# An adaLN decode block on one core: a quarter of w2's last row loaded apart, and all of w2 in calls of 128 columns

## The chip, the core and the metric

The kernel runs on one core of one Trainium2 chip. The metric is the device time of one execution in microseconds (us), the median of the runs shown. The kernel before took 235.53 us (three runs, 235.41 to 235.98). The profile is of one execution; its times count from its first instruction.

The engines are named as in the profile: PE (matrix multiply) with PEld (its loading of weights), DVE, ACT, POOL, and SP, which here only issues transfers. A "call" below is one matmul of the program. In float32 the chip runs each call as two passes, so the profile counts two matmuls for a call.

## The reference

One decode step for two rows: an attention branch over a window of 4096 cached positions, and a feed-forward branch, both modulated by a condition `c`. Cut to what matters:

```python
mod = (silu(c) @ w_mod).reshape(2, 6, 1, 512)
sa, ca, ga, sb, cb, gb = (mod[:, i] for i in range(6))
h = layernorm(x) * (1 + ca) + sa
x = x + ga * attention(h, k_cache, v_cache, wq, wo)   # 32 query heads, 8 KV heads of 128,
                                                      # the last 4096 of 32768 positions
h = layernorm(x) * (1 + cb) + sb
x = x + gb * (silu(h @ w1) @ w2)                      # w1: 512 x 1792, w2: 1792 x 512
```

`x` is 2 x 1 x 512. All arrays are float32.

## The kernel before

Everything is streamed once from HBM through `slots`, a ring of eight buffers of 128 partitions x 4096 numbers (`stream`, line 70). SP issues the loads in program order: w_mod, x, wq, then for eight steps the K and V rows of a pair of heads (`load_pair`, two buffers, 4 MB each), then wo in two loads, w1 in two, and w2 in four (`load_runs`). A load is issued when its buffer is free, so SP mostly waits, for the last reader of the buffer. `fetch(s)` asks for K of step s and V of step s - 1.

A step s: `keys` turns K on DVE, `scores` multiplies on PE, `maxima` and `exponentials` make the softmax, `turn` turns the weights, `weighted` multiplies V, `collect` adds the heads into `o_all`. `tc.keep_in_program_order` (`inorder`) fixes the order of the instructions it wraps; the rest is placed by a scheduler. `qbd[0]` and `qbd[1]` hold the queries, spread out over 128 x 1024 numbers; `qbd[0]` serves the heads of steps 0 to 3 alone.

The sums over heads are divided by the softmax's denominator (`rx`, `lp`, `rl`, `on`, lines 516 to 538), turned (`oTn`), and multiplied by wo. `busy(n)` puts n matmuls whose result nobody reads on PE.

The feed-forward branch at the end is what the change touches:

- The hidden vector has 1792 numbers, on 128 partitions x 14 (`T2`). `uT` holds it after SiLU, ready as weights: slice tt is `uT[:, tt, :]`, 32 columns of which two (columns 0 and 16) carry the two rows of the batch.
- Partition p of w2's buffers holds rows 14 p to 14 p + 13 of w2, so slice tt of w2 is one row of 512 on each partition. "The last row" is slice 13. The four loads bring slices 0 to 7, 8 to 10, 11 to 12, and 13.
- Slices 0 to 7 (`WIDE`) run as calls of 512 columns (line 663), four column groups of PE side by side: slice tt goes to partitions 32 g to 32 g + 31 of the bank `yw`, g = tt % 4. Each group then holds the sum of two slices over all 512 columns.
- Slices 8 to 10 run as four calls of 128 columns each (line 673): the g-th quarter of the columns goes to partitions 32 g and up of the bank `y`. This is the layout that the rest of the kernel has: batch row b's g-th quarter stands on partition 32 g + 16 b.
- `gather(y, yw, ...)` (lines 548 to 560, called in line 680) brings the wide sums into that layout: ACT and DVE copy one half of `yw` each to SBUF, and four calls with `id4` (which adds the four groups) put the quarters into `y`.
- Slices 11 to 13 run as calls of 64 columns into two banks `yl[0]`, `yl[1]` (line 688).
- DVE then multiplies `y` by `gb` and adds x1 (`yp`, lines 696 and 697), multiplies the two `yl` by `gb` (line 701), adds both (line 704), and SP stores `yo` (line 706).

PSUM banks are named by a tag; tag D has two buffers, used in turn.

Of the kernel before, what the change touches and what calls it, by code (L numbers as in the profile page):

```python
# [19 lines left out]
RING = 8  # L20


@with_exitstack
def adaln_block(
# [82 lines left out]
    for b in range(B):  # L107
# [55 lines left out]
        odd, ident.rearrange("p (a r) -> p r a", r=2), axis=AX.X, op=ALU.add  # L163
    )
# [434 lines left out]
    T2, WIDE = F // P, 8  # L599
# [60 lines left out]
    yw = bank("D", "acc_yw")  # L660
    for tt in range(WIDE):
        g = tt % 4
        inorder(nc.tensor.matmul(  # L663
            yw[32 * g : 32 * g + 32, :],
            uT[:, tt, :],
            w2t[tt],
            start=(tt < 4),
            stop=(tt >= WIDE - 4),
        ))
    y = bank("D", "acc_y")[:, :P]  # L670
    for tt in range(WIDE, 11):
        for g in range(4):
            inorder(nc.tensor.matmul(  # L673
                y[32 * g : 32 * g + 32, :],
                uT[:, tt, :],
                w2t[tt][:, g * P : (g + 1) * P],
                start=(tt == WIDE),
                stop=False,
            ))
    gather(y, yw, "acc_y_sb", False, True)  # L680
# [3 lines left out]
    for tt in range(11, T2):  # L684
        for h in range(2):
            for g in range(4):
                lo = g * P + h * H
                inorder(nc.tensor.matmul(
                    yl[h][32 * g : 32 * g + 32, :],
                    uT[:, tt, :],  # L690
                    w2t[tt][:, lo : lo + H],
                    start=(tt == 11),
                    stop=(tt == T2 - 1),
                ))
# [39 lines left out]
```

## Time and profile before

| | |
|---|---|
| median of three runs | 235.53 us |
| span of the profiled execution (first to last instruction) | 233.7 us |
| mean TensorE clock granted | 0.934 of full |
| read from HBM | 97.53 MB, 417 GB/s over the span |
| busy share: PE, PEld, DVE, ACT, POOL | 69%, 18%, 49%, 12%, 5% |
| last instruction of DVE ends, output's store is issued | 231.1 us |

The page gives no total time for the profiled execution; the median of the runs lies 1.8 us above its span, which is what lies around it. In the page's slices each digit is a tenth. A row of the chain of waits gives its start, its length and what ran or was waited for. A row of the timeline merges neighbouring instructions of one line: start, length from the first start to the last end, engine, line, operation, output <- inputs, shape, count, and in brackets the idle time before it with what ended it. "SPq" is the time at which SP issues a transfer. w1 and w2 both read as "in_B_w" there.

The chain of waits of the whole execution, by engine (share of the span):

```profile
DMA 60%; issue 17%; DVE 14%; PE 6%; POOL 1%; POOLq 0%; SPq 0%; ACT 0%; DVEq 0%
```

Waiting for transfers makes up most of it.

### The profile page before, as it was taken

Reading aid. Unit: us, or ns where it says so; the run is one execution under the profiler, and the core shown is the slowest. Engines: PE = TensorE matmul, PEld = TensorE weight load, DVE = VectorE, ACT = ScalarE, POOL = GpSimd, SP = SyncE. Lnnn points to the kernel's source line nnn. Section 1 sums busy time; section 2 is a strip of 40 time slices with the busy share of each in tenths; the row PEclk is TensorE's granted clock in tenths of the full one; section 3 lists DMA queues with packets and bytes.
Section 4 is the critical chain, followed back from the end, with each engine's and each line's share of the span. In section 5 each row is a group of like instructions: output and inputs, shape, how many; then the busy total and the mean of one; then the engine's idle time right before and its main releaser. Section 6 shows DMA issues by size and latency. Waiting matters only on the chain.

```text
span 233.7 us, 2571 instructions
## 1 busy us (share of the span) xinstructions
PE 160.2 (69%) x1070; PEld 43.1 (18%) x1070; DVE 115.6 (49%) x179; ACT 28.5 (12%) x64; POOL 10.6 (5%) x35
## 2 busy tenths in 40 slices
PE   0005916959577839787689759758769777869784
PEld 0001401211111111221111202201112122314223
DVE  3004140178795758696197189249559540101232
ACT  1100210000311120120210201111030031002020
POOL 8600010000000000000000000000000000000000
PEclk9999975879979997999979988999997999999999
DMA  7998998999999999999999999999999999989991
GB/s 269 446 520 381 426 471 359 440 443 428 415 421 449 440 443 421 421 423 449 443 437 426 415 429 449 437 437 429 404 444 443 437 423 471 446 362 427 423 412 57
DMA packets 3795, 97.68 MB, mean 418 GB/s; under 512 B 433, under 2 KB 457, under 8 KB 969
## 3 DMA queue, kind: packets, MB, share of 16 engines
q1 hardware_dynamic: 3768, 97.53, 97.2%
q8 instruction: 8, 0.13, 0.2%
q14 instruction: 3, 0.02, 0.0%
q10 hardware_dynamic: 16, 0.00, 0.0%
HBM read 97.53 MB, written 0.00 MB: 417 GB/s over the span
## 4 chain that ended last, share of the span: by engine, by line
DMA 60%; issue 17%; DVE 14%; PE 6%; POOL 1%; POOLq 0%; SPq 0%; ACT 0%; DVEq 0%
DMA slots<-in_A_k_cache_dram 22%; DMA slots<-in_A_wq_dram 14%; DMA slots<-in_B_w_dram 12%; DMA slots<-in_A_v_cache_dram 12%; DVE kT L363 11%; PE q L304 3%; PE o L450 2%; DVE zp L422 1%; PE acc_yw L663 1%; DVE xp L420 1%; PE acc_y L673 0%; DVE xc L102 0%; POOL qg L321 0%; DVE qT L317 0%; PE acc_y L554 0%
## 5 line engine op out<-in xcount | busy, mean ns | idle before, releaser
L363 DVE STREAM_TRANSPOSE kT<-slots 128x1024 f32<-128x1024 f32 x64 | 73.7, 1210 | 22.9 <-DMA slots<-in_A_k_cache_dram 22.8
L376 PE MATMUL s<-kT,qbd 128*32 128x512 f32 x256 | 68.5, 703 | 17.9 <-DVE kT L363 17.0
L450 PE MATMUL o<-slots,ptb 128*32 128x512 f32 x256 | 29.1, 595 | 2.2 <-DMA slots<-in_A_v_cache_dram 2.2
L376 PEld LDWEIGHTS s<-kT,qbd 128*32 128x32 f32 x256 | 9.8, 113 | 66.9 <-DVE kT L363 62.9
L271 PE MATMUL m_a<-slots,scT 128*32 128x256 f32 x32 | 4.4, 507 | 20.4 <-DVE scT L263 20.4
L304 PE MATMUL q<-slots,hq_T 128*32 128x512 f32 x64 | 9.7, 773 | 7.4 <-DMA slots<-in_A_wq_dram 7.4
L450 PEld LDWEIGHTS o<-slots,ptb 128*32 128x32 f32 x256 | 7.7, 109 | 16.7 <-issue 16.6
L406 ACT COPY bias<-bp 128x1 f32<-128x1 f32 x8 | 1.3, 159 | 75.8 <-PE bp L404 75.8
L386 DVE TENSOR_REDUCE mx<-s 128x1 f32<-128x512 f32 x8 | 5.5, 691 | 9.6 <-PE s L376 9.6
L567 PE MATMUL junk<-quad,id 128*32 128x512 f32 x22 | 10.2, 596 | 0.0
L437 ACT ACTIVATE ptb<-pT,odd 128x256 f32<-128x256 f32 x16 | 6.7, 472 | 26.0 <-PE pT L429 26.0
L422 DVE TENSOR_TENSOR zp<-xp,quarter 128x1024 f32<-128x1024 f32 x8 | 9.8, 1225 | 0.2
L429 PE MATMUL pT<-zp,mix 128*32 128x256 f32 x64 | 5.8, 438 | 4.0 <-DVE zp L422 4.0
L317 DVE STREAM_TRANSPOSE qT<-q 128x512 f32<-128x512 f32 x2 | 1.4, 717 | 13.5 <-PE q L304 12.0
L581 PE MATMUL acc_o<-slots,oTn 128*32 128x512 f32 x56 | 6.2, 593 | 2.3 <-DMA slots<-in_A_wo_dram 2.3
L460 ACT COPY ob<-o 128x512 f32<-128x512 f32 x8 | 4.7, 586 | 24.4 <-PE o L450 24.4
L552 DVE COPY acc_o_sb<-acc_o 128x256 f32<-128x256 f32 x1 | 0.4, 425 | 14.1 <-ACT acc_o_sb L551 14.1
L388 PE MATMUL mT<-ident,mx 128*1 128x128 f32 x16 | 3.0, 270 | 6.3 <-DVE mx L386 6.3
L420 DVE STREAM_TRANSPOSE xp<-pr 128x512 f32<-128x512 f32 x8 | 5.5, 685 | 3.4 <-ACT pr L408 3.4
L257 DVE STREAM_TRANSPOSE cT<-xc 128x128 f32<-128x128 f32 x1 | 0.4, 401 | 13.7 <-DMA xc<-in_c_dram 13.7
L274 PE MATMUL m_sp<-slots,scT 128*32 128x512 f32 x32 | 7.2, 730 | 0.0
L468 PE MATMUL o_all<-ob,selh 128*64 128x128 f32 x64 | 5.9, 313 | 0.8 <-ACT ob L460 0.8
(140 smaller groups left out, 93.7 us busy)
## 6 DMA issues: line engine op xcount, KB each, us to landing
slots<-in_A_k_cache_dram SPq DMA_DIRECT2D x8, 4096.0 KB, 27.6
slots<-in_A_v_cache_dram SPq DMA_DIRECT2D x8, 4096.0 KB, 27.7
slots<-in_w_mod_dram SPq DMA_DIRECT2D x1, 6144.0 KB, 17.2
slots<-in_A_wo_dram SPq DMA_DIRECT2D x1, 6144.0 KB
slots<-in_B_w_dram SPq DMA_DIRECT2D x1, 2688.0 KB
slots<-in_A_wo_dram SPq DMA_DIRECT2D x1, 2048.0 KB, 29.5
slots<-in_B_w_dram SPq DMA_DIRECT2D x1, 2048.0 KB
slots<-in_B_w_dram SPq DMA_DIRECT2D x1, 896.0 KB
```

Of the source, the lines that this page charges most:

```text
L274: nc.tensor.matmul(m_sp[r, :], scT[:, k, :], cd[:, g], start=(k == 0), stop=(k == 3))
L304: nc.tensor.matmul(q_ps[n][32 * g : 32 * g + 32, :], hq_T[:, k, :], wv[:, n, g], start=(k == 0), stop=(k == 3),)
L363: inorder(nc.vector.transpose(kT[s, j][:, 32 * c : 32 * c + 32, :], kt[s].rearrange("p (n j r) -> p j n r", j=4, r=32)[:, j, 32 * c : 32 * ...
L376: inorder(nc.tensor.matmul(s_ps[s][r : r + 32, :], qbd[h // 4][:, h % 4, b, j, :], kT[s, j][:, 32 * c : 32 * c + 32, e:32:2], start=(j == ...
L420: inorder(nc.vector.transpose(xp, pr[s]))
L422: inorder(nc.vector.tensor_mul(zp, xp[:, None, :, 0:16].to_broadcast([P, 4, 16, 16]), quarter[:, :, None, None].to_broadcast([P, 4, 16, 16 ...
L429: inorder(nc.tensor.matmul(tp[32 * i : 32 * i + 32, :], mix.rearrange("p v e -> p (v e)"), zp.rearrange("p y t x -> p (y t) x")[:, :, 4 * ...
L437: inorder(nc.scalar.activation(ptb[s % 2][:, :, e, :], tp.rearrange("p (w z) -> p w z", z=16), AF.Copy, scale=odd[:, e : e + 1],))
L450: inorder(nc.tensor.matmul(o_ps[s][r : r + 32, :], ptb[s % 2][:, w].rearrange("p e z -> p (e z)"), vt[s].rearrange("p (c w m f d) -> p c f ...
L468: inorder(nc.tensor.matmul(o_all[r : r + 64, :], selh[:, m, lo : lo + 2 * HQ], o_sb[s][:, m * DH : (m + 1) * DH], start=(s == 0 and m < 2) ...
L567: inorder(nc.tensor.matmul(junk[0:32, :], id4, quad.rearrange("p m y -> p (m y)"), start=True, stop=True,))
L581: inorder(nc.tensor.matmul(acc[32 * g : 32 * g + 32, :], oTn[:, q, :], wot[q], start=(q < 4), stop=(q >= 24),))
```

## The change

Three things, all in the feed-forward branch and its loads.

**A quarter of the last row is loaded apart.** Columns 384 to 511 of slice 13 (128 numbers on each of 128 partitions, 64 KB) no longer come with the last load, which becomes 128 x 384. They go to a tile `far` in the memory of `qbd[0]`, which is free after step 3, and which POOL clears first. Rows of partitions 8 to 127 go there in eight loads of 15 rows (`move`), to three partitions of `far` each with five rows one behind the other (`far[:, j]`, j = 0 to 4): 24 partitions, 0 to 11 and 32 to 43. The rows of partitions 0 to 7 (`own`) go to `far[:8, 5]`. The moves are issued between the K and V loads of the last steps and the loads of wo; the row of `own` after them.

**Their products have a bank of their own.** The rows no longer stand on the partitions of their hidden numbers, so these are moved too: DVE writes slice 13 of `uT` into six pairs of columns, each masked to the partitions that `far[:, j]` took (`uj`, with the mask `slot`), one call with the 0/1 matrix `away` carries them to the 24 and 8 partitions (`up`), DVE copies that into `uF`, and six calls multiply `uF[:, j]` by `far[:, j]` into the bank `yf`, in four column groups. ACT copies `yf` to SBUF, and one call with `id4` adds the four groups into the last quarter of `y`. `away` and `slot` are made at the start by POOL and DVE.

**All slices from 0 to 10 run in calls of 128 columns** (`narrow`) into `y`; `yw` and its `gather` are gone. The load of slices 0 to 7 is split in two of four slices. The calls of `up`, `yf` and `id4` stand between the narrow ones.

```diff
+NE, NR, NJ = 3, 4, 5
...
+    own = P - 2 * NR * NJ * NE
+    away, slot = const([P, 48], "away"), const([P, NJ + 1], "slot")
+    nc.gpsimd.memset(away, 0.0)
+    for h in range(2):
+        nc.vector.tensor_reduce(
+            away[:, 32 * h : 32 * h + NE * NR].rearrange("p (e r) -> p e r", e=NE),
+            ident[:, own + 60 * h : own + 60 * h + 60].rearrange(
+                "p (r j e) -> p e r j", r=NR, j=NJ
+            ),
+            axis=AX.X,
+            op=ALU.add,
+        )
+    nc.vector.tensor_add(away[:, :own], away[:, :own], ident[:, :own])
...
+    T2, WIDE = F // P, 8
+    w2p = w2.rearrange("(p t) e -> p t e", t=T2)
+    spare = qbd[0].rearrange("p s b j c -> p (s b j c)")
+    NS = NJ + 1
+    far = spare[:, : NS * P].rearrange("p (j m) -> p j m", j=NS)
+    uF = spare[:, NS * P : NS * (P + 32)].rearrange("p (j n) -> p j n", j=NS)
+    uj = spare[:, NS * (P + 32) : NS * (P + 32 + B)].rearrange("p (j b) -> p j b", j=NS)
+    moves = [(h, r) for h in range(2) for r in range(NR)]
+
+    def move():
+
+        if len(moves) == 2 * NR:
+            nc.gpsimd.memset(spare, 0.0)
+        h, r = moves.pop(0)
+        lo = own + 60 * h + NJ * NE * r
+        nc.sync.dma_start(
+            far[32 * h : 32 * h + NE * NR, :NJ].rearrange("(e r) j m -> e r j m", r=NR)[:, r],
+            w2p[lo : lo + NJ * NE, T2 - 1, D - P :].rearrange("(j e) m -> e j m", e=NE),
+        )
...
             kt[s] = load_pair(k_cache, s)
+            if s > STEPS // 2 + 1:
+                move()
         if s > 0:
             vt[s - 1] = load_pair(v_cache, s - 1)
+            if s > STEPS // 2:
+                move()
...
         wt = load_runs(wo, 32, lo, hi)
+        move()
         wot.extend(wt[:, q, :] for q in range(hi - lo))
+    nc.sync.dma_start(far[:own, NJ], w2p[:own, T2 - 1, D - P :])
...
-    for lo, hi in ((0, WIDE), (WIDE, 11), (11, 13), (13, T2)):
+    wide = stream(1).rearrange("p (q e) -> p q e", e=D)
+    for lo in (0, WIDE // 2):
+        nc.sync.dma_start(wide[:, lo : lo + WIDE // 2, :], w2p[:, lo : lo + WIDE // 2, :])
...
+    w2l = stream(1)[:, :D]
+    nc.sync.dma_start(w2l[:, : D - P], w2p[:, T2 - 1, : D - P])
...
-    yw = bank("D", "acc_yw")
-    for tt in range(WIDE):
...
-    gather(y, yw, "acc_y_sb", False, True)
+    nc.vector.tensor_mul(
+        uj,
+        uT[:, T2 - 1, 0:32:16][:, None, :].to_broadcast([P, NS, B]),
+        slot[:, :, None].to_broadcast([P, NS, B]),
+    )
...
+    narrow(0)
+    up = bank("C", "up")[:48, : NS * B]
+    inorder(nc.tensor.matmul(up, away, uj.rearrange("p j b -> p (j b)"), start=True, stop=True))
+    inorder(nc.vector.tensor_copy(
+        uF[:48, :, 0:32:16], up.rearrange("p (j b) -> p j b", b=B)
+    ))
+    for tt in range(1, 4):
+        narrow(tt)
+    yf = bank("D", "acc_yf")[:, :P]
+    for j in (4, 5, 0, 1, 2, 3):
+        g = j % 4
+        inorder(nc.tensor.matmul(
+            yf[32 * g : 32 * g + 32, :],
+            uF[:, j, :],
+            far[:, j, :],
+            start=(j in (4, 5, 2, 3)),
+            stop=(j < 4),
+        ))
+    yfs = once.tile([P, P], F32, tag="wide", name="acc_yf_sb")
+    inorder(nc.scalar.copy(yfs, yf))
+    for tt in range(4, WIDE):
+        narrow(tt)
+    inorder(nc.tensor.matmul(y[3 * 32 :, :], id4, yfs, start=False, stop=False))
+    for tt in range(WIDE, 11):
+        narrow(tt)
...
     for tt in range(11, T2):
+        n = 4 if tt < T2 - 1 else 3
```

Three places of the order in which the engines' instructions stand. First PE at the end of the program, before (`acc_yw` and `acc_y` are the banks `yw` and `y`, `acc_l` the two `yl`; a row is a run of equal calls with output <- inputs and the shape of one):

```order
L567 MATMUL junk<-quad,id_58 32x512 x3
L663 MATMUL acc_yw<-slots,uT 32x512 x8
L673 MATMUL acc_y<-slots,uT 32x128 x12
L554 MATMUL acc_y<-acc_y_sb,id_58 32x128 x4
L688 MATMUL acc_l_1106<-slots,uT 32x64 x4
```

and in the changed kernel (`qbd` is here `uj`, `uF` and `far`, `acc_yf` the bank `yf`):

```order
L615 MATMUL junk<-quad,id_58 32x512 x3
L724 MATMUL acc_y<-slots,uT 32x128 x4
L734 MATMUL up<-qbd_159,away 48x12
L724 MATMUL acc_y<-slots,uT 32x128 x12
L743 MATMUL acc_yf<-qbd_159 32x128 x6
L724 MATMUL acc_y<-slots,uT 32x128 x16
L754 MATMUL acc_y<-acc_yf_sb,id_58 32x128
L724 MATMUL acc_y<-slots,uT 32x128 x12
L765 MATMUL acc_l_1155<-slots,uT 32x64 x4
```

The eight wide calls and the four of the gathering became 32 narrow ones, with `up`, `yf` and one call of `id4` between them; the last slice at L765 has three calls for each half in place of four.

Second SP, from the loads of wo on, before. In brackets stands what a load waits for: an engine, or one of eight completion counters (HW0 to HW7) that the loads of the program take in turn, each waiting for the load that had its counter before, or for one that filled the same buffer:

```order
L93 DMA slots<-in_A_wo_dram 128x12288 [waits DMAHW3_49,DMAHW4_49,DVE_49,PE_49]
L93 DMA slots<-in_A_wo_dram 128x4096 [waits DVE_49]
L93 DMA slots<-in_B_w_dram 128x5376 [waits DMAHW5_49,PE_49]
L93 DMA slots<-in_B_w_dram 128x1792 [waits DMAHW6_49,PE_49]
L93 DMA slots<-in_B_w_dram 128x4096 [waits PE_49]
L93 DMA slots<-in_B_w_dram 128x1536 [waits DMAHW7_49,PE_49]
L93 DMA slots<-in_B_w_dram 128x1024 [waits PE_49]
L93 DMA slots<-in_B_w_dram 128x512 [waits PE_49]
```

and in the changed kernel (`qbd` is `far`):

```order
L94 DMA slots<-in_A_wo_dram 128x12288 [waits DMAHW5_49,DMAHW7_49,DVE_49,PE_49]
L385 DMA qbd_159<-in_B_w_dram 3x5x128 [waits DMAHW6_49]
L94 DMA slots<-in_A_wo_dram 128x4096 [waits DVE_49]
L385 DMA qbd_159<-in_B_w_dram 3x5x128 [waits DMAHW0_49]
L557 DMA qbd_159<-in_B_w_dram 8x128 [waits DMAHW1_49]
L94 DMA slots<-in_B_w_dram 128x5376 [waits DMAHW2_49,PE_49]
L94 DMA slots<-in_B_w_dram 128x1792 [waits DMAHW3_49,PE_49]
L650 DMA slots<-in_B_w_dram 128x2048 [waits DMAHW4_49,PE_49]
L650 DMA slots<-in_B_w_dram 128x2048 [waits DMAHW5_49,PE_49]
L94 DMA slots<-in_B_w_dram 128x1536 [waits DMAHW6_49,PE_49]
L94 DMA slots<-in_B_w_dram 128x1024 [waits DMAHW7_49,PE_49]
L658 DMA slots<-in_B_w_dram 128x384 [waits DMAHW0_49,PE_49]
```

Two moves and the row of `own` stand among the loads of wo and w1, the counters shift, and the loads of w2 now wait for counters too: HW5 and HW7 are those of the two loads of wo, HW6 and HW0 those of the two moves shown. Six more moves stand before, one behind each of the last two K loads and the last four V loads.

Third PE between the last two steps of the attention, before (`bp` carries the maxima of step 7, `o` is `weighted`, here of step 6, `pT` belongs to `turn` of step 7, `lp` sums the denominators):

```order
L404 MATMUL bp_860<-negscale,mrow_146 128x1
L450 MATMUL o_866<-slots,ptb_149 32x512 x16
L429 MATMUL pT_889<-zp_887,mix 32x256 x4
L525 MATMUL lp<-ones,rx 64x1 x2
```

and in the changed kernel:

```order
L450 MATMUL bp_875<-negscale,mrow_154 128x1
L573 MATMUL lp<-ones,rx 64x1 x2
L496 MATMUL o_881<-slots,ptb_157 32x512 x16
L475 MATMUL pT_904<-zp_902,mix 32x256 x4
```

The scheduler now puts `lp`, which waits for `rx` of step 7 on DVE, ahead of `weighted` of step 6.

More of the change, by code (lines that the diff above doesn't have):

```diff
@@ L163, in adaln_block @@
         odd, ident.rearrange("p (a r) -> p r a", r=2), axis=AX.X, op=ALU.add
+    )
[12 more added lines that the diff above has]
+    nc.vector.tensor_add(away[:, :own], away[:, :own], ident[:, :own])
+    nc.vector.tensor_reduce(slot[:, NJ:], ident[:, :own], axis=AX.X, op=ALU.add)
+    nc.vector.tensor_reduce(
+        slot[:, :NJ],
+        ident[:, own:].rearrange("p (hr j e) -> p j hr e", j=NJ, e=NE),
+        axis=AX.XY,
+        op=ALU.add,
     )
@@ L659, in adaln_block, with narrow @@
     nc.vector.tensor_mul(uT[:, :, 0:32:16], z, sg)
-    yw = bank("D", "acc_yw")
-    for tt in range(WIDE):
[L662 to L669, printed above, removed]
+    nc.vector.tensor_mul(
+        uj,
+        uT[:, T2 - 1, 0:32:16][:, None, :].to_broadcast([P, NS, B]),
+        slot[:, :, None].to_broadcast([P, NS, B]),
+    )
     y = bank("D", "acc_y")[:, :P]
-    for tt in range(WIDE, 11):
+    def narrow(tt):
         for g in range(4):
```

14 lines of the change are left out of this document (8 added, 6 removed).

## The prediction

> **What bounds the kernel now.** I read the slices first, then stretches of the end, the loads, and last the chain of waits. The page's row of the sixteen DMA engines in 40 slices, and the stretches (us, then busy us and counts of PE, PEld, DVE, ACT and POOL, granted clock, DMA share, GB/s):
>
> ```profile
> DMA  7998998999999999999999999999999999989991
> 2.00:226.00 224.00, 156.15 (x974) 40.87 (x974) 113.80 (x172) 28.18 (x63) 9.17 (x28) 0.93 1.00 429
> 226.00:227.60 1.60, 1.13 (x12) 0.50 (x16) 0.00 (x0) 0.00 (x0) 0.00 (x0) 1.00 1.00 410
> 227.60:228.20 0.60, 0.60 (x8) 0.00 (x0) 0.00 (x0) 0.00 (x0) 0.00 (x0) 1.00 0.80 321
> 228.20:228.60 0.40, 0.40 (x16) 0.31 (x16) 0.00 (x0) 0.09 (x1) 0.00 (x0) 1.00 0.47 189
> 228.60:229.10 0.50, 0.50 (x26) 0.48 (x16) 0.18 (x1) 0.28 (x1) 0.00 (x0) 1.00 0.50 197
> 229.10:229.60 0.50, 0.49 (x15) 0.23 (x12) 0.24 (x1) 0.00 (x0) 0.00 (x0) 1.00 0.45 143
> 229.60:230.00 0.40, 0.40 (x34) 0.40 (x32) 0.15 (x1) 0.00 (x0) 0.00 (x0) 1.00 0.01 5
> ```
>
> The transfers bound it: share 1.00 at 429 GB/s from 2 to 226 us, 26.8 GB/s for each of 16 engines. No compute that leaves the stream's bytes alone is worth anything before 226 us. The end is uneven: from 228.2 to 229.6 the share is 0.45 to 0.50, so half the engines have finished and the others run 1.4 us more. That late half sets the last landing, and the early half has 1.4 us of room. The loads and queues (issues with KB each and us to landing; packets, MB, share of 16 engines' span):
>
> ```profile
> slots<-in_B_w_dram SPq DMA_DIRECT2D x1, 256.0 KB, 17.3
> L93 SPq DMA_DIRECT2D slots<-in_B_w_dram x6: 328/328/328, 190.2 to 212.7; - x6
> q1 hardware_dynamic: 3768, 97.53, 97.2%
> q8 instruction: 8, 0.13, 0.2%
> q10 hardware_dynamic: 16, 0.00, 0.0%
> ```
>
> The last 256 KB are issued at 212.7 and land 17.3 us later, at 230.0. A source of the unevenness is visible: eight instruction blocks of 16 KB took 0.2% of 16 x 233.7 us, 0.93 us each, and each can only hold up the engine that fetches it. Which engines are late, no row says. The end of the chain of waits (start, us, what):
>
> ```profile
> 226.34 0.14 issue
> 226.47 1.92 PE acc_yw L663 x16
> 228.40 0.78 PE acc_y L673 x24
> 229.18 0.20 PE acc_y L554 x4
> 229.39 0.44 PE acc_y L554 x4
> 229.85 0.30 DVE yp L696
> 230.18 0.29 DVE yp L697
> 230.47 0.35 DVE yo L701 x2
> ```
>
> Two paths meet at L701. One is this chain, through the gathering, ready at 230.47. The other is the last landing at 230.0 and L688's last slice behind it, which the next rows end at 230.51. They are level, so shortening one alone gains nothing.
>
> **The change part by part.** Rows of the timeline (start, us, engine and line, count, idle before):
>
> ```profile
> 214.24 1.08 PE L590 MATMUL ao<-slots,oTn 128*32 128x128 f32 x32
> 217.13 0.38 PE L616 MATMUL mean_b<-ks,mean 128*128 128x2 f32 x2 [0.55 <-DVE ks L614]
> 225.32 0.20 DVE L659 TENSOR_TENSOR uT<-z,sgh 128x28 f32<-128x28 f32 x1
> 226.47 1.92 PE L663 MATMUL acc_yw<-slots,uT 128*32 128x512 f32 x16 [0.82 <-DMA slots<-in_B_w_dram]
> 228.32 0.86 PE L673 MATMUL acc_y<-slots,uT 128*32 128x128 f32 x24
> 228.51 0.37 ACT L551 COPY acc_y_sb<-acc_yw 128x256 f32<-128x256 f32 x1 [3.80 <-PE acc_yw L663]
> 229.54 0.97 PE L688 MATMUL acc_l<-slots,uT 128*32 128x64 f32 x47
> ```
>
> *Calls of 128 columns, no gathering.* A wide slice costs 1.92/8 = 0.24 us, a narrow one 0.86/3 = 0.29 with its drain, or 1.08/4 = 0.27; so eight slices cost 2.2 in place of 1.9. But they start sooner: uT is ready at 225.52, PE waits for the 2 MB load until 226.47, and its first half, now a load of its own, lands some 1 MB / 429 GB/s = 2.4 us before. New on PE: `up` (like L616, 0.38), six far calls (as 1.5 narrow slices, 0.4) and one call of id4 (0.1 to 0.3). From 225.6 PE runs 2.2 + 0.4 + 0.4 + 0.2 = 3.2 us to 228.8, then slices 8 to 10 (0.86) to 229.6 at the latest; by the shorter 0.22 between slices that the 24 matmuls of L673 allow, 229.2. Before, y stood at 229.83. The `yp` steps (0.30 + 0.29) end at 229.8 to 230.2 in place of 230.47: **this path drops out by 0.3 to 0.6 us.** The new copies hide behind narrow slices: DVE's 48x12 copy (0.2, like L659) and ACT's 128x128 copy (at most L551's 0.37) each have three or four slices, 0.8 us or more, in front of their reader. Uncovered, they cost 0.2 and 0.4 us, within the 0.3 to 0.6 that path has.
>
> *A quarter of the last row leaves the last load.* 256 KB become 192, on each engine 16 KB become 12: 4 KB / 26.8 GB/s = 0.15 us earlier. Against it: 512 bytes more on eight engines (0.02), and the split of the 2 MB load, which makes 8 KB packets of 16 KB ones and one more completion per engine. The trace does not show that price; its bounds are 0 and one completion like q10's packets, whose 0.0% means under 1.9 us for 16, 0.12 each. I take 0.05. Last landing: 0.15 - 0.02 - 0.05, some **0.1 us earlier**; bounds -0.01 and 0.15.
>
> *The eight moves.* Packet counts show how many engines a load uses. Twenty-six loads of 128 rows with a completion on 16 engines make 26 x 144 = 3744; x and the output, with eight rows each on four engines, add 2 x 12 = 24: q1's 3768. The c loads of two rows make q10's 16 = 4 x (2 + 2). So a load whose outer size is 2 or 4 uses that many engines, and one of 3 should use three: each gets 8 x 5 = 40 packets of 512 bytes, 20 KB, 0.76 us at 26.8 GB/s. If these engines belong to the early half, 1.4 us of room takes it; from 1.4/40 = 35 ns a packet on it no longer does (19 ns by the rate, under 120 by q10). I take nothing, and keep 0.7 for the case that one belongs to the late half.
>
> The Trainium skill, "DMA: Bandwidth & Descriptors", section "Why a DMA increments its semaphore by 16 and not by 1", says the engine count is the largest up to 16 that divides both sides' slowest dimension, and that they are the lowest-numbered ones; the counts agree with the first half, and no row shows the second. Spread over all 16 by another rule, the bytes would cost 0.15 us everywhere and cancel the gain.
>
> *Queues.* SP issues ten more loads, 0.33 to 0.73 us each by these rows, in waits of 76.8 us for buffers, with loads outstanding 17 to 34 us:
>
> ```profile
> L113 SPq DMA_DIRECT2D xc<-in_A_x_dram x1: 732/732/732, 2.6 to 2.6; - x1
> SPq L82 <- DVE kT L363: 76.8, 7, 13.7
> DMA to landing us min/median/max: 17.2/23.4/33.9
> 209.34 3.71 SPq L93 DMA_DIRECT2D slots<-in_B_w_dram  x3
> ```
>
> The order shows new completion waits: the second half of w2's wide load waits for wo's first (HW5), the load of slices 11 and 12 for wo's second (HW7). Behind each on SP stand the later w2 loads. wo's loads are read by PE from 208.2 on (next rows) and slice loads were issued from 209.3 to 212.7 anyway; 2 to 3 us later still leaves w1 and w2 queued, 17 us of landing time. Nothing. The first move waits for POOL's memset of `qbd[0]` (1.83/2 = 0.92 us by L212), and that for the last scores of step 3; behind it stands the K load of step 6. The V load ahead of it waits for weighted(2), which PE runs after those scores, so the memset is done or nearly: nothing, uncovered 0.9 us of SP, not of the stream.
>
> ```profile
> 6.18 1.83 POOL L212 MEMSET qbd<- 128x1024 f32 x2
> 3.20 0.27 DVE L145 TENSOR_REDUCE sixth<-ident 128x8 f32<-128x128 f32 x1
> 17.78 0.40 DVE L257 STREAM_TRANSPOSE cT<-xc 128x128 f32<-128x128 f32 x1 [13.68 <-DMA xc<-in_c_dram]
> 186.22 0.38 PE L404 MATMUL bp<-negscale,mrow 1*128 1x1 f32 x2 [0.52 <-DVE mrow L397]
> 186.52 3.64 PE L450 MATMUL o<-slots,ptb 128*32 128x512 f32 x32
> 188.27 0.15 DVE L518 TENSOR_TENSOR rx<-rowsum,selg 128x32 f32<-128x32 f32 x1
> 193.72 3.64 PE L450 MATMUL o<-slots,ptb 128*32 128x512 f32 x32 [2.16 <-DMA slots<-in_A_v_cache_dram]
> 208.24 4.07 PE L581 MATMUL acc_o<-slots,oTn 128*32 128x512 f32 x36 [2.33 <-DMA slots<-in_A_wo_dram]
> ```
>
> *The moved `lp`* now holds PE from 186.6 until rx ends at 188.42, and weighted(6) behind it: 1.9 us late. The 2.16 us wait for the last V load takes that in, or leaves 0.3 us, and the 2.33 us wait for wo the rest. The setup (four reductions and an addition, at most 0.3 us each by L145, 1.5 in all) lies in DVE's 13.68 us wait for c: nothing; without that wait it would delay scT, not the stream.
>
> **Sum.** The end follows the last landing, 0.1 us earlier, and a last slice of 12 matmuls in place of 16 (a quarter of 0.97/3, 0.08, of which the half before the first L701 counts, 0.04). Span 233.7 - 0.1 to 0.15 = 233.6. The median lies 1.8 us above the span; with the same 1.8 the median goes from 235.53 to **235.4**.
>
> **The rivals.** *One of the three engines belongs to the late half, or small packets cost over 35 ns.* For it: half the engines are late and no row names them. Against it: eight of sixteen are early, and late ones may come from instruction blocks, which need not fall on these three. Price 0.76 us at the end less the 0.1 gained, up to 1.2 at 30 ns a packet: 236.2 to 236.6, **236.3**. It decides from the first such engine whose end passes 229.6. Chance 0.17.
>
> *The landing is not the limit* and the whole 0.6 us of the gathering comes off: against it stands the landing at 230.0, which allows only its own shift; 234.9, with a late half that also shrinks 234.7. Chance 0.06.
>
> *Small loads stop all engines.* Each of nine would hold the stream as long as SP's issue, 0.33 to 0.73: 3 to 6.6 us, 240. Against it: x and c went in amid a share of 0.9 and more. The Trainium skill, same page, section "Bandwidth", calls transfers under 64 KB descriptor-dominated, 0.68 us for 4 KB, an estimate of 6 us for nine. Chance 0.02.
>
> *It does as said, within noise:* 0.75, spread 235.1 to 235.8 by the bounds above and the 0.5 us between the runs shown.
>
> **How the numbers follow.** Within 0.3% (0.7 us, about what a measurement can tell from no change): the forecast, most of the second rival, and the mild third of the first: 0.75 + 0.03 + 0.05 = 0.83. Slower: 0.12 + 0.02 = 0.14. Faster: 0.03. The range, 235.0 to 236.3, takes the forecast and the lower half of the first rival.
>
> **What would show it.** q1 with 3768 + 144 + 8 x 18 + 16 = 4072 packets; the first narrow call at 225.6 and not behind a load; y's last matmul before 229.7 and `yp` done before the last slices; the last landing at 229.9. A share of 0.2 or less that lasts from 229.6 to 230.5 would mean that moves sit on late engines. A share well under 1.00 before 226 us, or PE waiting for far or w2's second half, would make the prediction wrong.

## The result, and the profile after

| | before | after |
|---|---|---|
| median | 235.53 us (235.41 to 235.98) | 237.29 us (235.98 to 237.96, six runs) |
| ratio to before, of the means | | 1.0063, 95% interval 1.004 to 1.0086 |
| span of the profiled execution | 233.7 us | 233.9 us |
| time less span, run by run | 1.65 to 1.89 (105 runs beside the experiments below, median 1.81) | 2.08, 2.08, 3.07, 3.46, 3.51, 3.56 |

The change is slower, by 1.8 us between the medians. The forecast of 235.4 and its upper end, 236.3, are missed. The last row of the table is the surprise: each run lists its time and its span, and most of the loss stands between the two, in a part of the time that the page doesn't draw. Every kernel below is therefore read in two pieces, span and time less span.

First what is in the span. The page of the changed kernel, its span and its queues (packets, MB, share of 16 engines' span), and the six stretches at the end with the columns as before:

```profile
span 233.9 us, 2702 instructions
...
q1 hardware_dynamic: 4072, 97.53, 97.2%
q8 instruction: 8, 0.13, 0.2%
q14 instruction: 3, 0.02, 0.0%
```

```profile
226.00:227.60 1.60, 1.60 (x58) 1.57 (x58) 0.17 (x1) 0.00 (x0) 0.00 (x0) 1.00 1.03 420
227.60:228.20 0.60, 0.60 (x28) 0.52 (x20) 0.00 (x0) 0.27 (x1) 0.00 (x0) 1.00 0.85 341
228.20:228.60 0.40, 0.40 (x19) 0.36 (x17) 0.00 (x0) 0.00 (x0) 0.00 (x0) 1.00 0.71 271
228.60:229.10 0.50, 0.50 (x20) 0.24 (x11) 0.00 (x0) 0.00 (x0) 0.00 (x0) 1.00 0.73 267
229.10:229.60 0.50, 0.01 (x1) 0.02 (x1) 0.39 (x2) 0.00 (x0) 0.00 (x0) 1.00 0.31 114
229.60:230.00 0.40, 0.39 (x29) 0.40 (x33) 0.19 (x1) 0.00 (x0) 0.00 (x0) 1.00 0.00 0
```

The share from 228.2 to 229.1 rose from 0.47 and 0.50 to 0.71 and 0.73, and from 229.1 to 229.6 it fell from 0.45 to 0.31: the late DMA engines now have less left to do at the end. No row names the engines that took the moved bytes. The timeline of the same stretch:

```profile
225.65 0.42 PE L724 MATMUL acc_y<-slots,uT 128*32 128x128 f32 x8
226.30 0.17 DVE L735 COPY qbd<-up 48x12 f32<-48x12 f32 x1 [0.43 <-PE up L734]
227.62 0.27 ACT L751 COPY acc_yf_sb<-acc_yf 128x128 f32<-128x128 f32 x1 [2.83 <-PE acc_yf L743]
228.24 0.86 PE L724 MATMUL acc_y<-slots,uT 128*32 128x128 f32 x24
229.17 0.29 DVE L773 TENSOR_TENSOR yp<-acc_y,mod_sp 128x128 f32<-128x128 f32 x1 [2.70 <-PE acc_y L724]
229.50 0.29 DVE L774 TENSOR_TENSOR yp<-yp,x 128x128 f32<-128x128 f32 x1
229.61 0.87 PE L765 MATMUL acc_l<-slots,uT 128*32 128x64 f32 x44 [0.50 <-DMA slots<-in_B_w_dram]
230.42 0.36 DVE L778 TENSOR_TENSOR yo<-acc_l,mod_sp 128x64 f32<-128x64 f32 x2 [0.63 <-PE acc_l L765]
```

The path through `y` ends at 229.79 (L774) and is out of the way; PE now stands idle for 0.50 us ahead of slices 11 to 13, until the load of the first two of them lands (229.47 by the trace's records). What is left is the landing and the tail behind it. Issues of the output's store, before and after, from the timelines:

```profile
231.11 0.63 SPq L706 DMA_DIRECT2D out_dram<-yo  x1
```

```profile
231.06 0.64 SPq L783 DMA_DIRECT2D out_dram<-yo  x1
```

The store is issued 0.05 us earlier, where 0.1 to 0.15 had been forecast for the span. Yet the span ends 0.13 us later (233.86 against 233.73 by the traces), so something behind the store grew. SP's waits after 231.8, before and after (in all, times, longest):

```profile
SPq L730 <- DMA out_dram<-yo: 0.7, 1, 0.7
SPq L730 <- PEq L730: 0.6, 2, 0.4
```

```profile
SPq L807 <- DMA out_dram<-yo: 1.0, 1, 1.0
SPq L807 <- PEq L807: 0.6, 2, 0.4
```

The wait for the store is 0.3 us longer, though the store lands no later: it begins earlier. At its end SP checks the eight completion counters in a fixed order, two counters or a counter and an engine at a time: HW2; HW3 and HW1; HW4 and HW0; HW5; HW6; HW7. The store takes the counter whose turn it is. Before, it was load 32 of the program (28 of SP, 4 of ACT) and had HW7, which is looked at last. With ten loads more it is load 42 and has HW1, looked at second; four waits of about 0.06 us each then still follow its landing.

Then what lies behind the span. The DMA view of the stretch from 233.95 to 240 us, before and after:

```profile
DMA packets 1, 0.01 MB, mean 1 GB/s; under 512 B 0, under 2 KB 0, under 8 KB 0
## 3 DMA queue, kind: packets, MB, share of 16 engines
q14 instruction: 1, 0.01, 0.5%
```

```profile
DMA packets 2, 0.02 MB, mean 4 GB/s; under 512 B 0, under 2 KB 0, under 8 KB 0
## 3 DMA queue, kind: packets, MB, share of 16 engines
q8 instruction: 1, 0.02, 1.0%
q14 instruction: 1, 0.01, 0.5%
```

After the program's last recorded instruction one more 16 KB block of instructions is fetched on q8, from 236.24 to 237.20. Before, q8 had nothing left to fetch. That q8 carries PE's program is seen in e1 below, which adds calls on PE and nothing else: its page counts nine blocks on q8, and before eight. The change makes PE's program longer: 561 calls in place of 535, four instruction records each.

### The profile page after: what moved, and what is told of

It is laid out like the page before. It is cut to its first block, busy times and chain, and to the rows that moved or that the text cites. A ratio compares the mean times of both kernels' runs of the same rounds, so it can differ in the third digit from the quotient of the medians.

```text
span 233.9 us, 2702 instructions
## 1 busy us (share of the span) xinstructions
PE 164.3 (70%) x1122; PEld 44.1 (19%) x1122; DVE 116.1 (50%) x185; ACT 28.4 (12%) x64; POOL 11.6 (5%) x37
## 3 DMA queue, kind: packets, MB, share of 16 engines
q1 hardware_dynamic: 4072, 97.53, 97.2%
## 4 chain that ended last, share of the span: by engine, by line
DMA 68%; DVE 19%; PE 8%; ACT 1%; issue 1%; SPq 0%; ACTq 0%; POOL 0%; DVEq 0%; POOLq 0%
DMA slots<-in_A_k_cache_dram 43%; DVE kT L409 15%; DMA slots<-in_A_wo_dram 13%; DMA slots<-in_B_w_dram 7%; DMA xc<-in_c_dram 6%; PE s L422 4%; PE m_sp L296 2%; DVE zp L468 2%; PE m_a L293 1%; DVE xp L466 1%; ACT L454 1%; ACTq L110 0%; DVE sgc L249 0%; ACT pr L454 0%; PE acc_l L765 0%
## 5 line engine op out<-in xcount | busy, mean ns | idle before, releaser
L422 PE MATMUL s<-kT,qbd 128*32 128x512 f32 x256 | 69.9, 677 | 16.7 <-DVE kT L409 15.5
L496 PE MATMUL o<-slots,ptb 128*32 128x512 f32 x256 | 32.3, 650 | 0.1
L326 PE MATMUL q<-slots,hq_T 128*32 128x512 f32 x64 | 9.2, 740 | 7.7 <-DMA slots<-in_A_wq_dram 7.7
L615 PE MATMUL junk<-quad,id 128*32 128x512 f32 x22 | 11.7, 669 | 0.0
L475 PE MATMUL pT<-zp,mix 128*32 128x256 f32 x64 | 5.2, 397 | 3.9 <-DVE zp L468 3.7
L629 PE MATMUL acc_o<-slots,oTn 128*32 128x512 f32 x56 | 7.0, 594 | 0.0
L296 PE MATMUL m_sp<-slots,scT 128*32 128x512 f32 x32 | 6.6, 712 | 0.0
L514 PE MATMUL o_all<-ob,selh 128*64 128x128 f32 x64 | 5.3, 285 | 1.1 <-ACT ob L506 1.1
```

Of the source, the lines that this page charges most:

```text
L296: nc.tensor.matmul(m_sp[r, :], scT[:, k, :], cd[:, g], start=(k == 0), stop=(k == 3))
L326: nc.tensor.matmul(q_ps[n][32 * g : 32 * g + 32, :], hq_T[:, k, :], wv[:, n, g], start=(k == 0), stop=(k == 3),)
L422: inorder(nc.tensor.matmul(s_ps[s][r : r + 32, :], qbd[h // 4][:, h % 4, b, j, :], kT[s, j][:, 32 * c : 32 * c + 32, e:32:2], start=(j == ...
L496: inorder(nc.tensor.matmul(o_ps[s][r : r + 32, :], ptb[s % 2][:, w].rearrange("p e z -> p (e z)"), vt[s].rearrange("p (c w m f d) -> p c f ...
L615: inorder(nc.tensor.matmul(junk[0:32, :], id4, quad.rearrange("p m y -> p (m y)"), start=True, stop=True,))
L629: inorder(nc.tensor.matmul(acc[32 * g : 32 * g + 32, :], oTn[:, q, :], wot[q], start=(q < 4), stop=(q >= 24),))
```

## The experiments

All are compared with runs of the kernel before on the same chip. "Rest" is time less span, median of the runs. The kernel before had 235.38 to 235.50 us, span 233.60 and rest 1.81.

| kernel | PE calls | time | span | rest | ratio (95%) |
|---|---|---|---|---|---|
| after | 561 | 237.29 | 234.10 | 3.27 | 1.0063 (1.004 to 1.0086) |
| e1: before, 26 calls more | 561 | 235.32 | 233.60 | 1.70 | 0.9998 (0.9989 to 1.0007) |
| e2: moves, wide calls kept | 541 | 236.06 | 234.00 | 2.15 | 1.0035 (1.0022 to 1.0048) |
| e3: after, wo all wide | 549 | 235.83 | 233.80 | 2.05 | 1.0015 (1.0006 to 1.0025) |
| e4: narrow calls alone | 555 | 235.80 | 233.80 | 1.93 | 1.001 (1.0001 to 1.002) |
| e5: after, 6 calls more | 567 | 235.82 | 233.75 | 2.03 | 1.002 (1.0011 to 1.0029) |
| e6: before, 24 calls more | 559 | 235.35 | 233.60 | 1.75 | 0.9999 (0.999 to 1.0008) |
| e7: loads of the change alone | 535 | 235.85 | 233.95 | 1.92 | 1.0023 (1.0011 to 1.0035) |
| e8: e3, c's loads merged | 549 | 235.52 | 233.50 | 2.02 | 1.0006 (0.9997 to 1.0015) |
| e9: before, 21 calls more | 556 | 235.48 | 233.70 | 1.76 | 0.9997 (0.9988 to 1.0007) |
| e10: before, 23 calls more | 558 | 235.37 | 233.65 | 1.73 | 0.9994 (0.9984 to 1.0003) |
| e11: setup of the change alone | 535 | 235.43 | 233.60 | 1.81 | 1.0 (0.999 to 1.0009) |
| e12: after, 1 call fewer | 560 | 236.22 | 234.20 | 2.03 | 1.0042 (1.0026 to 1.0058) |
| e13: after, 1 call more | 562 | 237.09 | 233.85 | 3.25 | 1.0073 (1.0059 to 1.0087) |
| e14: e5, c's loads merged | 567 | 235.59 | 233.50 | 2.05 | 1.0005 (0.9997 to 1.0014) |
| e15: before, 8 tiny loads more | 535 | 235.40 | 233.70 | 1.76 | 0.9998 (0.9989 to 1.0007) |

### Parts of the change, one at a time

e1 adds only calls, as small as they come, to the kernel before:

```diff
     busy(6)
+    for _ in range(26):
+        inorder(nc.tensor.matmul(
+            junk[0:32, 0:1], id4, quad[:, 0, 0:1], start=True, stop=True
+        ))
```

> The kernel before with 26 more PE calls of one column (104 instructions, as many as the change adds) in PE's wait for wo; nothing else. Theory A (PE's instructions: a longer program ends in another block of instructions, fetched after the last instruction of the span): span 233.7 as before, time 236.7 to 237.5, and an instruction packet of 16 KB after the span. Theory B (SP's ten more loads lengthen the end of the program): 235.5. Theory C (late landings of the loads in executions without a profile): 235.5.

e2 has the moves, the bank of their own and the shorter last load, but runs slices 0 to 7 in wide calls and gathers them:

```diff
-    narrow(0)
+    for tt in range(4):
+        broad(tt)
...
+    gather(y, yw, "acc_y_sb", False, True)
```

> The moves, the row of own and the far bank of the change, but slices 0 to 7 in calls of 512 columns with the gathering and one load, as before: 541 PE calls (before 535, after 561). A: 541 is only 24 instructions over before, so 235.3 to 235.7 with a time 1.8 above the span. B and C: 236.7 to 237.5, as after, since all the loads of the change are there.

e3 is the changed kernel, with the last four rows of wo in wide calls too, which takes 12 calls out:

```diff
-    for q in range(28):
+    for q in range(32):
...
-    gather(ao, acc, "acc_o_sb", False, True)
+    gather(ao, acc, "acc_o_sb", True, True)
```

> The changed kernel with the last four rows of wo in calls of 512 columns too, which saves 12 PE calls (549 in place of 561). A: 235.3 to 235.6 if 549 calls end short of the block's boundary, else about 237 as after. B and C: about 237, as after.

e4 is the kernel before with narrow calls and no gathering, its loads as they were:

```diff
-    for tt in range(WIDE, 11):
+    for tt in range(11):
...
-    gather(y, yw, "acc_y_sb", False, True)
```

> The kernel before with slices 0 to 10 in calls of 128 columns and no gathering, loads untouched: 555 PE calls, the wide load in one piece. A: about 237 if 555 calls end past the boundary, else 235.5, with the time less the span at 3 or at 1.8 accordingly. B and C: 235.5 and 1.8.

e1 speaks against the plain form of theory A: a program of 561 calls costs nothing by itself. But e3 took 1.5 us off by 12 calls, with rests between 1.99 and 2.10 in all ten runs, which speaks against B and C: they had it at about 237. None of the three had e2's 236.06 with a rest of 2.15 (235.3 to 235.7 by A, 236.7 to 237.5 by B and C). The traces differ in where the ninth block is fetched. In e1 it came at 230.55, inside the span, while DVE and the store were still to come; in the changed kernel behind the span; in e2, e3 and e4 not at all. Neither half of the change reaches 237, so the big loss is no sum of its parts. e4 shows no gain from dropping the gathering, as forecast for a path that is only level with the landing; its span is even 0.2 us longer, and the cause of that stays open.

### Where a block of PE's instructions begins

e5 makes PE's work longer to make the kernel faster: six one-column calls more in the changed kernel, written as in e1.

> The changed kernel with six one-column calls more on PE ahead of the output projection (567 calls, 24 instruction records more). Time less span of the kernels so far, by their runs: before 1.80, with 26 small calls 1.70, narrow calls alone 1.93, moves with wide calls 2.15, moves with 549 calls 2.04; the changed kernel 2.08 in two runs and 3.07 to 3.56 in four. Theory A2 (one block of 256 of PE's instructions begins so near to the program's last instruction that it is fetched after the span, and the end waits for it): 24 instructions more put the start of that block ahead of the last matmul; the fetch stands within the span, time less span is 2.0 to 2.2 in every run, and the time is 236.0 to 236.3. Theory B2 (the end grows with the number of PE's instructions, or of SP's loads, or is a matter of chance in a kernel with both parts): time less span stays at 3.0 to 3.6 in most runs, and the time is 237.2 to 237.8.

235.82, with a rest of 2.00 to 2.15 in all ten runs: theory A2's number on the rest, a little under its time. Six useless calls gain 1.5 us. Its page has nine blocks in the span, and the DMA view behind the span (from 233.95 on) has lost the packet on q8:

```profile
q8 instruction: 9, 0.15, 0.2%
```

```profile
DMA packets 1, 0.01 MB, mean 1 GB/s; under 512 B 0, under 2 KB 0, under 8 KB 0
## 3 DMA queue, kind: packets, MB, share of 16 engines
q14 instruction: 1, 0.01, 0.5%
```

The next three try to bring the late fetch about in the kernel before, with 24, 21 and 23 calls of e1's kind.

> The kernel before with 24 one-column calls more on PE instead of 26 (559 calls; 8 instruction records fewer than with 26, where the ninth block was fetched in the span at 230.55, right ahead of the last instructions; nothing else is changed). Theory A2 (a block that begins at the program's last instructions is fetched after the span, whatever the kernel does otherwise): time less span is 2.7 to 3.6, with a fetch of 16 KB after the span, and the time is 236.4 to 237.2; or, should 8 instructions not do, no ninth fetch at all and a time less span of 1.7 to 1.95. Theory B2 (the late fetch needs the loads of the change): time less span 1.7, the time 235.3, and the ninth fetch within the span as with 26.

> The kernel before with 21 one-column calls more on PE (556 calls; with 24 the ninth block of instructions was fetched in the span at 230.47, with 2267 of 2270 records begun, and time less span was 1.70 to 1.80; narrow calls alone, with 555 calls, had no ninth fetch and 1.93, once 2.61). Theory A2 (the late fetch is a matter of where a block begins, and of nothing else in the change): at one of the two counts 21 and 23 the block begins behind the instructions at which PE waits for the end, and is fetched after the span; that kernel has a time less span of 2.6 to 3.6 in most runs and a time of 236.2 to 237.2. Theory B3 (it takes the change's loads as well): 1.65 to 1.95 in every run, and 235.3 to 235.5, at both counts.

> The kernel before with 23 one-column calls more on PE (558 calls). The two theories as for 21: by A2 one of the two counts gives a time less span of 2.6 to 3.6 and a time of 236.2 to 237.2, the other 1.65 to 1.95 and 235.3 to 235.5; by B3 both give 1.65 to 1.95.

It came at none of these counts: rests of 1.67 to 1.93 throughout. With 23 and 24 the ninth block was fetched at 230.81 and 230.47, with 21 there was none. So by number B3 is right as far as these go. Count 22 between them wasn't run, and e9 and e10 leave room for a late fetch in that one count alone. A late fetch without the change's loads was not shown. One of e4's ten runs, with 555 calls and none of these loads, has a rest of 2.61 where the other nine have 1.89 to 1.96; it was not the profiled one, so whether it is such a fetch stays open.

e12 and e13 ask the same of the changed kernel itself, one call fewer and one more:

```diff
-    busy(6)
+    busy(5)
```

> The changed kernel with one of its six warm-up calls ahead of the output projection left out (560 calls, 4 instruction records fewer than in the changed kernel). Time less span so far, by calls: with the change's loads 2.04 at 549, 2.08 or 3.1 to 3.6 at 561, 2.04 at 567; without them no rise at 555, 556, 558, 559 and 561. Theory A3 (a late fetch takes a block that begins within a few instructions of the last one): one call fewer puts it past the program's last instruction, or leaves it at the edge; time less span 2.0 to 2.2 in most or all runs, the time 235.9 to 236.2. Theory B4 (with the change's loads the late fetch comes over a wide stretch of counts): 3.0 to 3.6 in most runs, the time 237.2 to 237.7.

> The changed kernel with one one-column call more (562 calls, 4 records more). Theory A3: the block begins four instructions earlier against the program's end, so that PE has passed its start when it waits for the end; the ninth fetch stands in the span, time less span is 2.0 to 2.2, the time 235.9 to 236.2. Theory B4: 3.0 to 3.6 in most runs, 237.2 to 237.7.

With 560 calls the rest is 2.01 to 2.09 in all four runs, with 562 it is 3.18 to 3.43 in all four. Behind the span, the profile of e12 and then of e13:

```profile
q14 instruction: 1, 0.01, 0.5%
```

```profile
q8 instruction: 1, 0.02, 1.1%
q14 instruction: 1, 0.01, 0.6%
```

At 560 no ninth block, at 561 a late one in four runs of six (by the rest: 3.07 to 3.56 against 2.08), at 562 a late one always, at 567 one inside the span. Theory A3 was right that the window is a few instructions wide and wrong on its far side: 562 still lies in it. B4's wide stretch ends within one call below and five above. Two profiled executions had the late packet (after and e13); there it ends at 237.20 and 237.21 and the times are 236.97 and 236.98, 0.23 apart in both (the two scales need not start at the same moment). The end of the time follows the packet, which fits an end that waits for this fetch; no row shows the wait itself.

The Trainium skill, "Runtime: NRT & Kernel Launch", section "Instruction fetch mechanics", says that an engine's instructions are fetched ahead in blocks of 16 KiB, 256 instructions, and that crossing a block's bound is mostly hidden. The trace agrees for the eight blocks of PE in the span, some 0.9 us each beside running calls. It does not for the one behind the last instruction, where no call is left to run beside it: 1.2 us in the medians of e13 and e12 (3.25 against 2.03). Nor does the size hold everywhere: the packets on q14, which move with DVE's and SP's programs (below), are of 8 KB.

### The counter of the store

e8 is e3 with one load for each row of c in place of two, so that the store is load 40 and has HW7 again:

```diff
-        for lo in (0, 2):
-            nc.scalar.dma_start(
-                c_sp.rearrange("(g y) m -> g y m", g=4)[lo : lo + 2, 16 * b, :],
-                c[b].rearrange("(g m) -> g m", m=P)[lo : lo + 2],
-            )
+        nc.scalar.dma_start(
+            c_sp.rearrange("(g y) m -> g y m", g=4)[:, 16 * b, :],
+            c[b].rearrange("(g m) -> g m", m=P),
+        )
```

> The changed kernel with all of wo in wide calls (549 calls), and with each row of c loaded by one DMA in place of two: the loads are two fewer, so that the output's store gets the counter that SP's waits at the end look at last, as in the kernel before. Theory L (the place of the store's counter among those waits costs the span 0.06 for each wait that still follows): the span falls from 233.8 (median of ten runs of the same kernel with two loads for each row) to 233.5 to 233.6, and the time from 235.83 to 235.55 to 235.65, with time less span still at 2.04. Rival K (the waits behind the store's landing are hidden by what the other engines do at the end): span 233.8, time 235.8. By either it isn't faster than the kernel before by more than 0.1.

Span 233.50 against 233.80, rest unchanged, time 235.52: theory L. The trace's records of SP's waits at the end, start, end and what follows the landing, e3 on the left:

```
e3: store on HW1                     e8: store on HW7
231.513 231.530  HW2                 231.531 231.548  HW2
231.566 232.568  HW3, HW1: landing   231.585 231.612  HW3, HW1
232.603 232.631  HW4, HW0            231.646 231.674  HW4, HW0
232.667 232.695  HW5                 231.710 231.738  HW5
232.729 232.757  HW6                 231.772 231.800  HW6
232.788 232.816  HW7                 232.575 232.603  HW7: landing
233.542 233.559  last of SP          233.325 233.342  last of SP
```

The store is issued at 230.85 in e3 and 230.86 in e8, so nothing ahead of it differs. In e3 the landing's wait ends at 232.568 and SP's last record 0.99 us later; in e8 at 232.603 and 0.74 us later. Four waits of 0.06 us are the 0.25.

e14 puts both repairs into the changed kernel, six calls and c's loads merged:

> The changed kernel with both repairs: six one-column calls more (as in the run where time less span fell to 2.04) and one DMA for each row of c (so that the store has the counter that is waited for last). The sum of the parts: 235.82 of the first repair alone, less 0.25 for four waits behind the store, is 235.55 to 235.6, with span 233.45 to 233.55 and time less span 2.04: the span 0.1 to 0.15 shorter than that of the kernel before, as forecast for the last landing, and the time still 0.1 to 0.2 above it. If the repairs don't add, 235.8.

They add: 235.59, span 233.50, rest 2.05. Its store is issued a little sooner than before's and its span is 0.1 shorter in the medians, so this is what the change itself is worth:

```profile
230.99 0.64 SPq L786 DMA_DIRECT2D out_dram<-yo  x1
```

With the repairs the change is level with the kernel before (1.0005, 0.9997 to 1.0014). No version of the change beat it.

### The rest that stays: 0.25 us

Even repaired, the rest is 2.05 and not 1.81. e7 has only the loads, unread; e11 only the setup, with seven instructions more on DVE; e15 eight loads of 32 bytes, one in each place where the change has a move. The first lines below are common to e7 and e15, which differ in what `move` loads; e15's load follows.

```diff
+            if s > STEPS // 2 + 1:
+                move()
...
+        move()
```

> The kernel before with the loads of the change alone: the memset, the eight moves and the small load of 8 partitions are issued where the change issues them, and nothing reads them; w2's last row still comes whole, and all calls are as before. 65 KB more are loaded, and the output's store gets the counter that SP's waits at the end look at third. Theory M (SP's longer program is what lengthens time less span by 0.25 to 0.35, and the waits after the store's counter lengthen the span): time less span 2.05 to 2.2; span 233.9 to 234.1 (0.15 to 0.2 for the bytes, 0.2 for three waits behind the store instead of none); the time 236.0 to 236.3. Rival N (the longer time less span comes from the vector engine's or PE's longer programs): time less span 1.75 to 1.85, the time 235.7 to 235.9.

> The kernel before with the setup of the change alone, which nothing reads: one memset on POOL and seven instructions on the vector engine (the five of the change, and one of them twice more, so that the vector engine's program is as much longer as in the change); loads and calls as before. Theory V (time less span goes from 1.80 to 2.04 and more with the vector engine's longer program, whose instructions come in blocks as PE's do): time less span 2.0 to 2.15, the time 235.6 to 235.7. Theory M (it goes with the loads that SP issues; the loads alone gave 1.66 to 2.04, with a median of 1.92): 1.75 to 1.85, the time 235.4.

```diff
+        q = moves.pop(0)
+        nc.sync.dma_start(tiny[q : q + 1, :], w2[q : q + 1, :8])
```

> The kernel before with eight loads more on SP of 32 bytes each, issued where the change issues its eight moves, and read by nobody; the store keeps the counter waited for last. Theory M (time less span goes with the number of loads that SP issues): 1.9 to 2.1 instead of 1.80, span unchanged, the time 235.55 to 235.7. Rival (it takes the many small rows of the moves, or the longer programs of several engines together): 1.75 to 1.85, the time 235.4 to 235.5.

e11 gave 1.81 and e15 1.76, both at the kernel before: neither DVE's longer program nor eight loads more on SP do it by themselves. e7 gave 1.92, between the two theories, with runs from 1.66 to 2.04, and its span rose by 0.35 as M has it. So the change's loads bring a part, some 0.1 in the median; e4 shows 1.93 without any of them.

The traces go a step further. Behind e7's span two blocks of 8 KB are fetched on q14, where the kernel before has one:

```profile
q14 instruction: 2, 0.02, 0.8%
```

The end of the last such block, counted from the end of the span, beside the instructions recorded for SP and DVE and the rest of the same execution:

| kernel | SP | DVE | last block on q14 ends | rest |
|---|---|---|---|---|
| e1, e6, e10 | 61 | 192 | 1.10 to 1.22 | 1.70 to 1.71 |
| e9 | 61 | 192 | 1.01 | 1.86 |
| e4 | 61 | 191 | 1.43 | 1.90 |
| e11 | 61 | 199 | none behind the span | 1.79 |
| e15 | 71 | 192 | 1.23 | 1.84 |
| e7 | 75 | 192 | 2.21 | 1.97 |
| e2 | 75 | 200 | 2.39 | 2.15 |
| e3, e5, e8, e12, e14 | 76 to 77 | 198 to 199 | 2.00 to 2.15 | 2.04 to 2.12 |

Where SP has 75 records or more, a block ends 2.0 to 2.4 us behind the span and the rest is 1.97 to 2.15; with 61 or 71 none ends later than 1.43, and the rest is at most 1.90. (The changed kernel and e13 have such a block too, ending 2.13 and 2.18 behind the span and ahead of PE's late one.) e11's longer program on DVE moved the late block of the kernel before to 220.20, inside the span, and left the rest as it was. So what stays looks like a second late fetch, of SP's program as the first is of PE's: the change lengthens it by ten loads and six other records, and e15's eight loads fall short of the bound. This is read from traces that differ in more than SP's program; no run moved SP's count alone, so the cause is argued and not shown. Time before the first instruction counts in the rest too, and the profile has nothing of it.

## Why the prediction was wrong

**What bounds the kernel: right.** The share from 2 to 226 us is still 1.00:

```profile
2.00:226.00 224.00, 160.32 (x982) 40.70 (x982) 114.57 (x178) 28.15 (x63) 10.17 (x29) 0.93 1.00 428
```

**Narrow calls, no gathering: right, a little better.** The first narrow call runs at 225.65 (forecast 225.6), y's last matmul ends at 229.10 (229.2 to 229.6), `yp` at 229.79 against 230.47, 0.68 earlier where 0.3 to 0.6 stood. The copies took 0.17 and 0.27 us (0.2 and at most 0.37), hidden.

**A quarter of the last row: right in kind, near in size.** By the trace's records the last load lands at 229.88 (forecast 229.9), against 230.03 in the kernel before. The store's issue, behind it, came 0.05 earlier in the changed kernel and 0.12 in e14; 0.1 to 0.15 was the sum.

**Eight moves on three engines each: right.** q1 has the 4072 packets forecast, and the share falls to 0.00 by 229.6. The rival of a late engine had asked for a share of up to 0.2 that lasts to 230.5; it isn't there. The other two rivals, 234.9 and 240, found nothing either.

**Queues: right for the stream, wrong for the end.** SP's waits after the change:

```profile
SPq L650 <- DMA slots<-in_A_wo_dram: 8.6, 1, 8.6
...
SPq L94 <- DMA slots<-in_A_wo_dram: 2.4, 1, 2.4
```

These are the new waits for wo's two loads that the order showed, and the share of 1.00 says that they cost nothing. But the same step put ten more loads on SP down as "Nothing", while they moved the store from the last counter to the second: 0.25 us of span (e3 and e8, e5 and e14). The counters' turns stand in the order of SP above the prediction; it asked who waits for a load, and not who waits for the counters at the end.

**The moved `lp`: right that it costs nothing, too small in the delay.** It ran at 188.52, and `weighted(6)` began at 188.83 in place of 186.52, 2.3 us late where 1.9 stood. It also took 5.12 us in place of 3.64; the clock granted from 188.8 to 194.0 was 0.71, against 1.00 from 186.5 to 190.2 before.

```profile
188.52 0.38 PE L573 MATMUL lp<-ones,rx 128*64 128x1 f32 x4 [1.97 <-DVE rx L566]
188.83 5.12 PE L496 MATMUL o<-slots,ptb 128*32 128x512 f32 x32
```

The loads of w1, the first of which waits for the buffer that `weighted(6)` reads, were so issued 3.8 us later. Before, then after (a row starts with the first of them):

```profile
190.19 22.86 SPq L93 DMA_DIRECT2D slots<-in_B_w_dram  x6
```

```profile
193.99 3.72 SPq L94 DMA_DIRECT2D slots<-in_B_w_dram  x2
```

`weighted(7)` ran at 195.44 in place of 193.72, so the wait for V left 1.7 us of the delay and not 0.3. The rest of the account held: w1's two loads landed at 219.36 and 221.49 against 219.30 and 221.44, and the calls on wo began at 208.30 against 208.24.

**The sum: here it failed.** "The median lies 1.8 us above the span; with the same 1.8 the median goes from 235.53 to 235.4." The 1.8 was carried over as a constant. It is 1.81 in the kernel before, but 2.03 to 2.05 with the change's loads and calls, and 3.0 to 3.6 when PE's ninth block begins at its last instructions. With the measured terms, 233.60 - 0.10 (the change in the span, by e14) + 0.25 (counters) + 0.24 (the rest that stays) + 1.81 + 1.24 (late fetch: 3.27 less 2.03) makes 237.04; the median was 237.29. The difference lies in the span, 234.10 in the median where these terms give 233.75 (e5 has 233.75, e12 234.20, e13 233.85). The span of a run of the changed kernel goes from 233.9 to 234.4, and what makes it longer than e5's stays open. The rival that should have stood there is one of program length: PE's calls rise by 26, eight blocks had been fetched with the last at 229.32, and the next begins about where the longer program ends (in the kernel before between 556 and 558 calls, by e9 and e10). That the change has 561 calls and not 549 or 567 is bad luck: nothing in it aimed at that count, and a forecast would have had to hold both outcomes.

## What to carry to other kernels

Where a change of a per cent is wanted, split every run into span and time less span first; if the loss lies in the second, no view of the span will explain it. When a change adds calls or loads, look at the program's end as at any other stage: at how PE's last block of instructions falls (a few empty calls more or fewer move it; here one call or two decided over 1 us) and at which completion counter the last store takes (four small loads made two gave 0.25 us back).

## What the runs showed of the hardware

- PE's block of 16 KB begins in a window of a few instructions at the program's end, or it doesn't: 560 calls 236.22 us, 562 calls 237.09, 567 calls 235.82. At 561 the same program fell on either side from run to run, 235.98 and 236.18 or 236.97 to 237.96.
- Time less span stayed within 0.24 us in the kernel before (1.65 to 1.89 in 105 runs), but it is not the same from kernel to kernel: 1.70 to 3.27 in the medians here.
- Blocks of instructions of 8 KB come on q14, beside PE's on q8. In the profiled executions one that ended up to 1.43 us behind the span went with a rest of 1.90 at most, one that ended 2.0 to 2.4 us behind it with 1.97 to 2.15.
- A check of completion counters at the program's end costs SP 0.06 us each, and only those behind the last landing count.
